# A top-k attention and MLP kernel: output projection as seven half-size products, scores in three PSUM banks, first MLP layer in halves

## The chip, the cores and the metric

The kernel runs on one core of one Trainium2 chip. Its time is the device time of one execution in microseconds, median of several runs; lower is better. The engines are named as the profile names them: PE (matrix products; PEld its weight loads), DVE, ACT, POOL (GpSimd) and SP (which issues the DMAs here). Each works through its own queue in order.

## What is computed

Attention over q, k, v of shape (8, 8, 576, 64), where each query keeps its 32 largest scores, then an MLP of width 2048 over the 4608 x 512 result:

```python
scores = scale * np.matmul(q, k.transpose(0, 1, 3, 2))
kth = np.partition(scores, -top_k, axis=-1)[..., -top_k:-top_k + 1]
scores = np.where(scores >= kth, scores, -1000000000.0)
scores = scores - np.max(scores, axis=-1, keepdims=True)
attn = np.exp(scores)
attn = attn / (np.sum(attn, axis=-1, keepdims=True) + 1e-09)
x = np.matmul(attn, v).transpose(0, 2, 1, 3).reshape(B * S, H * D)
h = x @ w_in
g = h * (1.0 / (1.0 + np.exp(-1.702 * h)))
out = g @ w_out
```

## The kernel before

Work comes in 144 slots, 18 per batch. A slot is 128 queries of two heads at once (`t < NF`, 16 of the 18), or the last 64 queries of four heads (`t == NF`, two of the 18, side by side in a batch; they come first in odd batches and last in even ones). A slot goes through these steps, each a function of the slot's number `n`:

- `scores(n)` (line 221): matmuls of 64 rows of contraction for the two heads in turn, 576 keys each in two parts of 288, into two PSUM tiles `s_ps` of two banks each (the pool has two buffers, four banks). Two ACT copies (line 238) take them to `sc`.
- `topk(n)` (line 240): on the DVE, four rounds of `max` (line 247) and three of `match_replace` (line 250) for each head; 14 instructions.
- `bounds(n)` (line 261): two small POOL instructions that need the end of `topk(n)`.
- `exponentials(n)` (line 269): two Prelu (line 275) and two Exp (line 277) on ACT. `bounds` and `exponentials` together are called `soften`.
- `divide(n)` (line 282): a sum and a reciprocal on the DVE (lines 286, 288), issued after six of the next slot's 14 DVE instructions; then one head is scaled on ACT (line 294) and the other on POOL (line 295).
- `turn_main(n)` and `turn_ends(n)` (lines 318, 322): 8 transposes and 1 transpose on PE (line 306) into banks `tp`, each bank copied to `pt` by ACT (line 316). The pool `ps_t` has two banks for all of `tp` and `o`.
- `values(n)` (line 328): 20 half-width matmuls of attention by v into `o` (line 338; a `t == NF` slot has two `o`), copied by ACT into `xT`. Every fourth slot completes an `xT` of 128 tokens by 512; there are 36 of them.

The MLP of one `xT` is cut in four groups of four 128-wide blocks. `hidden()` (line 372) makes 16 matmuls (line 381) into the bank `ph`; `tanh` (line 393) is an ACT pass over `ph` and a copy of it to `h` (lines 398, 401); `gate` (line 405) makes `gT` from them on POOL (lines 411, 412); `project` (line 419) adds four matmuls of 512 columns (line 429) into the bank `po`, which ACT reads into `ob` after the fourth group (line 434), and SP sends out. Every float32 matmul is two instructions in the profile, a transpose is one.

The order on every engine is the order in which the program is written, under `manual_schedule` (line 640). Slots 0 to 9 run one by one in `slot`, with the weights being loaded and rounded in between; the rest runs in pairs `two_slots(n)` (line 572) for n = 10, 12, ..., 144:

```python
begin(first); soften(n - 1); tanh(aside); find(n); gate(aside)
prepare_some(); middle(n - 2); hidden()
begin(second); soften(n); tanh(aside); gate(aside)
prepare_some(); middle(n - 1); find(n + 1); prepare_some()
# then scores(n + 2), values(n - 2), values(n - 1), scores(n + 3)
prepare_some(); hidden()
```

Here `find` is `topk` with the `divide` of the slot before in it; `middle(m)` is three blocks of a projection, `turn_main(m)`, the fourth block, `turn_ends(m)`; `prepare_some` turns a loaded q or k of two heads (9 transposes for a q and a k, with ACT copies at lines 201 to 208); `begin` issues loads. One group of the first layer and one projection are done per slot; after n = 142 some are left over, which the calls at the end of the program finish.

Of the kernel before, what the change touches and what calls it, by code (L numbers as in the profile page):

```python
# [28 lines left out]
def kernel(  # L29
# [26 lines left out]

    nc = tc.nc
# [16 lines left out]
    FIRST = (TAIL, 0)  # L74
# [5 lines left out]
    SETTLED = 9  # L80
    assert D == 64 and 2 * TAIL == P and C == NP * P and C == PIECE and B % 2 == 0
# [3 lines left out]
    pool = lambda name, bufs, **kw: ctx.enter_context(tc.tile_pool(name=name, bufs=bufs, **kw))  # L85
    raws = pool("raws", 8)
    loads = pool("loads", 2)
# [10 lines left out]
    gtp = pool("gtp", 4)  # L98
    thp = pool("thp", 2)
    osp = pool("osp", 1)  # L100
    ps_s = pool("ps_s", 2, space=PSUM)
# [8 lines left out]


    pieces = [(c, g) for g in range(NG) for c in range(CC)] + [(None, f) for f in range(FC)]
    raw = {}

    def load_piece(n):
        c, g = pieces[n]
        if c is None:
            src = moe_w_out[g * P : (g + 1) * P, :]
        else:
            src = moe_w_in[c * P : (c + 1) * P, g * PIECE : (g + 1) * PIECE]  # L120
        raw[n] = raws.tile([P, 2 * PIECE], U32, name="raw")
        nc.sync.dma_start(raw[n][:], src.bitcast(U32))

    def round_piece(n):
# [9 lines left out]
        dst = wout[:, g, :] if c is None else win[:, c, g * PIECE : (g + 1) * PIECE]  # L134
        words = raw.pop(n)[:].rearrange("p (n w) -> p n w", w=2)
        low, high = words[:, :, 0], words[:, :, 1].bitcast(F32)
# [20 lines left out]

    def stay_warm(count, of=ident[:]):

        none = ps_p.tile([P, C], F32, name="none", tag="po")  # L160
        for i in range(count):
            nc.tensor.matmul(none[:, 0:P], lhsT=of, rhs=of, start=True, stop=True)

    def load(name, b, hp):
        src = q if name == "q" else k
        t = loads.tile([P, NF, 2, D], F32, name=f"{name}_l")
# [3 lines left out]
        if name == "q":  # L170
            loaded["ends", b, hp] = loads.tile([P, 2, D], F32, name="ends")
# [19 lines left out]
    def prepare(name, b, hp):  # L191
        src = loaded.pop((name, b, hp))


        before = 0 if name == "q" else TAIL
        dst = qkt.tile([P, S + before], F32, name=f"{name}_t")
# [4 lines left out]
        nc.scalar.mul(out=dst[:, before : before + FULL], in_=full[:], mul=scale)  # L201
        (qT if name == "q" else kT)[b, hp] = dst
        if name == "k":
# [3 lines left out]
            for to in (0, before + FULL):  # L207
                nc.scalar.copy(out=dst[:, to : to + TAIL], in_=ends[:, TAIL:P])
# [12 lines left out]
    def scores(n):  # L221
        b, t, hps = slots[n]
        ps = [ps_s.tile([P, 2, 512], F32, name="s_ps") for _ in range(2)]
        if t < NF:
            parts = [(i, 0, slice(0, P), slice(t * P, (t + 1) * P)) for i in range(2)]
        else:
            parts = [(i, p, slice(p * TAIL, (p + 1) * TAIL), slice(FULL, S)) for i, p in ((0, 0), (1, 1), (0, 1), (1, 0))]
        for c in range(2):
            for i, p, rows, cols in parts:
                on = slice(i * D, (i + 1) * D)  # L230
                nc.tensor.matmul(  # L231
                    ps[i][rows, c, 0:HALF],
                    lhsT=qT[b, hps[p]][on, cols],
                    rhs=kT[b, hps[p]][on, FIRST[i] + c * HALF : FIRST[i] + (c + 1) * HALF],
                )
        sc = st[n]["sc"] = scp.tile([P, 2, S], F32, name="sc")
        for i in range(2):
            nc.scalar.copy(out=sc[:, i, :].rearrange("p (c k) -> p c k", c=2), in_=ps[i][:, :, 0:HALF])  # L238
# [129 lines left out]
    hidden_at = {"g": 0}  # L368
# [3 lines left out]
    def hidden():  # L372
        if not ready:
            return
        xT, rows = ready[0]
        g = hidden_at["g"]
        ph = ps_h.tile([P, G, P], F32, name="ph")
        for i in range(G):
            f = g * G + i
            for c in range(CC):  # L380
                nc.tensor.matmul(  # L381
                    ph[:, i, :],
# [5 lines left out]
        to_gate.append((ph, g, rows))  # L388
        hidden_at["g"] = (g + 1) % NG
        if g == NG - 1:  # L390
            ready.pop(0)

    def tanh(aside):

        if to_gate:
            ph, g, rows = to_gate.pop()
            th = thp.tile([P, G, P], F32, name="th")
            nc.scalar.activation(th[:], ph[:], AF.Tanh, scale=0.851 / RAISE)  # L398
            if aside:
                h = raws.tile([P, G, P], F32, name="h", tag="raw")  # L400
                nc.scalar.copy(out=h[:], in_=ph[:])
                ph = h
            gated.append((th, ph, g, rows))

    def gate(aside):
        if not gated:
            return
        th, h, g, rows = gated.pop()
        gT = gtp.tile([P, G, P], F32, name="gT")
        if aside:  # L410
            nc.gpsimd.tensor_scalar(th[:], th[:], 1.0, None, op0=ALU.add)  # L411
            nc.gpsimd.tensor_tensor(out=gT[:], in0=th[:], in1=h[:], op=ALU.mult)  # L412
        else:
            nc.vector.scalar_tensor_tensor(
                out=gT[:], in0=th[:], scalar=1.0, in1=h[:], op0=ALU.add, op1=ALU.mult
            )
        to_project.append((gT, g, rows))

    def project(blocks):

        if blocks[0] == 0:
            proj["on"] = to_project.pop(0)
            if proj["on"][1] == 0:
                proj["po"] = ps_p.tile([P, C], F32, name="po")
        gT, g, rows = proj["on"]
        po = proj["po"]
        for i in blocks:
            f = g * G + i
            nc.tensor.matmul(  # L429
                po[:], lhsT=gT[:, i, :], rhs=wout[:, f, :], start=(f == 0), stop=(f == FC - 1)  # L430
# [249 lines left out]
```

## Time and profile before

| | |
|---|---|
| median of 3 runs | 1628.78 us (1628.63 to 1629.83) |
| profiled execution | 1632.4 us |
| its span, first to last instruction | 1630.6 us |
| PE clock granted, mean | 0.987 |
| DMA queues, mean rate | 35 GB/s |
| projection matmuls, L429 | 542.1 us busy, 1152 instructions |
| first-layer matmuls, L381 (`xT`) | 484.6 us busy, 4096 instructions |
| DVE max, L247 (two groups) | 609.9 and 202.2 us busy, 864 and 288 instructions |
| ACT score copies, L238 | 169.9 us busy, 288 instructions |

A busy row counts from an instruction's start to its end, and PE's instructions overlap: L429 has a mean of 594 ns where the next starts after some 430. The time that PE's work takes is therefore read from start to start. In the timeline a row is a start, a length, an engine, a line, an operation, the tiles out and in, the shape, the number of instructions, and the idle time before it with what ended it.

### The profile page before, as it was taken

The page shows a single profiled execution, that of the slowest core. Times are in us where ns is not written, and L with a number is a line of the kernel's source. Part 1 is how long each engine was busy: PE and PEld are TensorE (multiplying, and loading weights), DVE is VectorE, ACT ScalarE, POOL GpSimd, SP SyncE. Part 2 cuts the span into 40 slices and gives each one's busy share as a digit, 9 for nine tenths or more (in the row PEclk, how much of TensorE's full clock was granted, in tenths as well). Part 3 has the DMA queues.
Part 4 walks back from the last instruction along what each step waited for, and adds up shares of the span by engine and source line. Part 5 has one row for each costly group of instructions (what it writes and reads, how often), then busy time and mean ns, then how long its engine had stood idle before and what let it go on. Part 6 is the DMA issues. An engine that isn't in the chain of part 4 may idle for free.

```text
span 1630.6 us, 32137 instructions
## 1 busy us (share of the span) xinstructions
PE 1584.6 (97%) x12025; PEld 1184.1 (73%) x12025; DVE 1479.2 (91%) x3212; ACT 1155.9 (71%) x2449; POOL 754.1 (46%) x782
## 2 busy tenths in 40 slices
PE   7777999999999999999999999999999999999999
PEld 5665677777777777777777777777777777777776
DVE  6998999999999999999999998999999999999960
ACT  5896777777777776677777777777777777777761
POOL 2788344444444444444444444444444444444430
PEclk7898999999999999999999999999999999999999
DMA  7442001110001001110000100111000100000000
GB/s 209 124 137 76 22 22 29 30 43 16 22 15 44 22 23 29 29 37 22 22 15 23 35 17 15 30 30 44 15 22 15 43 22 23 22 8 7 8 8 14
DMA packets 100636, 56.61 MB, mean 35 GB/s; under 512 B 83584, under 2 KB 91776, under 8 KB 100480
## 3 DMA queue, kind: packets, MB, share of 16 engines
q1 hardware_dynamic: 100480, 54.55, 12.1%
q8 instruction: 95, 1.56, 0.4%
q14 instruction: 61, 0.50, 0.1%
HBM read 45.09 MB, written 9.44 MB: 33 GB/s over the span
## 4 chain that ended last, share of the span: by engine, by line
PE 88%; ACT 5%; DVE 4%; POOL 1%; issue 1%; SPq 0%; DMA 0%; POOLq 0%; ACTq 0%
PE ph L381 30%; PE po L429 29%; PE o L338 9%; PE s_ps L231 9%; PE tp L306 8%; DVE top L247 2%; DVE left L250 2%; PE tp L199 1%; ACT sc L238 1%; ACT pr L277 1%; ACT raw L146 1%; PE tp L308 1%; DVE wout L145 0%; ACT sc L275 0%; DMA raw<-in_moe_w_in_dram 0%
## 5 line engine op out<-in xcount | busy, mean ns | idle before, releaser
L247 DVE MAX8 top<-left 128x8 f32<-128x576 f32 x864 | 609.9, 747 | 0.0
L429 PE MATMUL po<-wout,gT 128*128 128x512 f32 x1152 | 542.1, 594 | 0.0
L381 PEld LDWEIGHTS ph<-xT,win 128*128 128x128 f32 x4096 | 467.5, 192 | 41.5 <-issue 40.8
L381 PE MATMUL ph<-xT,win 128*128 128x128 f32 x4096 | 484.6, 277 | 0.0
L250 DVE MATCH_REPLACE8 left<-top,left 128x576 f32<-128x576 f32 x576 | 423.4, 743 | 0.0
L295 POOL TENSOR_SCALAR pr<-pr,rden 128x576 f32<-128x576 f32 x135 | 233.4, 1729 | 356.0 <-ACT th L398 347.9
L411 POOL TENSOR_SCALAR th<-th 128x512 f32<-128x512 f32 x133 | 198.9, 1496 | 224.2 <-ACT th L398 224.2
L429 PEld LDWEIGHTS po<-wout,gT 128*128 128x128 f32 x1152 | 197.8, 191 | 142.3 <-issue 141.8
L275 ACT ACTIVATE sc<-sc,cut 128x576 f32<-128x576 f32 x288 | 208.1, 774 | 130.5 <-POOL cut L266 128.1
L316 ACT COPY pt<-tp 128x512 f32<-128x512 f32 (+1 forms) x432 | 193.2, 481 | 148.1 <-PE tp L306 141.0
L306 PEld LDWEIGHTS tp<-ident,pr 128*128 128x128 f32 x1215 | 145.7, 141 | 113.9 <-issue 65.8
L238 ACT COPY sc<-s_ps 128x576 f32<-128x576 f32 x288 | 169.9, 644 | 75.8 <-PE s_ps L231 75.4
L277 ACT ACTIVATE pr<-sc,low 128x576 f32<-128x576 f32 x288 | 219.2, 764 | 0.0
L247 DVE MAX8 top<-sc 128x8 f32<-128x576 f32 x288 | 202.2, 744 | 11.3 <-ACT sc L238 11.3
L250 DVE MATCH_REPLACE8 left<-top,sc 128x576 f32<-128x576 f32 x288 | 211.7, 743 | 0.0
L306 PE MATMUL tp<-ident,pr 128*128 128x128 f32 x1215 | 177.7, 273 | 9.0 <-ACT q_t L201 7.7
L231 PE MATMUL s_ps<-k_t,q_t 64*128 64x288 f32 (+1 forms) x1280 | 183.3, 433 | 0.9 <-ACT k_t L201 0.9
L412 POOL TENSOR_TENSOR gT<-th,h 128x512 f32<-128x512 f32 x133 | 169.8, 1277 | 11.1
L338 PE MATMUL o<-pt,v_l 128*64 128x128 f32 (+1 forms) x2560 | 158.9, 267 | 1.2 <-ACT pt L316 0.3
L338 PEld LDWEIGHTS o<-pt,v_l 128*64 128x64 f32 x2560 | 131.6, 138 | 31.3 <-ACT pt L316 15.8
L231 PEld LDWEIGHTS s_ps<-k_t,q_t 64*128 64x128 f32 (+1 forms) x1280 | 100.0, 178 | 59.6 <-issue 40.5
L266 POOL TENSOR_SCALAR cut<-top 128x2 f32<-128x2 f32 x144 | 38.2, 265 | 208.5 <-DVE top L247 206.8
(55 smaller groups left out, 1175.3 us busy)
## 6 DMA issues: line engine op xcount, KB each, us to landing
q_l<-in_q_dram SPq DMA_DIRECT2D x64, 128.0 KB, 2.9
k_l<-in_k_dram SPq DMA_DIRECT2D x64, 128.0 KB, 2.9
raw<-in_moe_w_in_dram SPq DMA_DIRECT2D x16, 512.0 KB, 5.1
v_l<-in_v_dram SPq DMA_DIRECT2D x32, 256.0 KB, 3.0
raw<-in_moe_w_out_dram SPq DMA_DIRECT2D x16, 512.0 KB, 3.3
out_dram<-ob SPq DMA_DIRECT2D x32, 256.0 KB, 2.3
ends<-in_q_dram SPq DMA_DIRECT2D x32, 32.0 KB, 2.4
ends<-in_k_dram SPq DMA_DIRECT2D x32, 32.0 KB, 2.6
```

Source lines behind the costliest of these rows:

```text
L231: nc.tensor.matmul(ps[i][rows, c, 0:HALF], lhsT=qT[b, hps[p]][on, cols], rhs=kT[b, hps[p]][on, FIRST[i] + c * HALF : FIRST[i] + (c + 1) * ...
L247: nc.vector.max(top[:, i, 8 * r : 8 * r + 8], (left if r else sc)[:, i, :])
L250: nc.vector.match_replace(left[:, i, :], top[:, i, 8 * r : 8 * r + 8], (left if r else sc)[:, i, :], LOWEST)
L275: nc.scalar.activation(sc[:, i, :], sc[:, i, :], AF.Prelu, bias=cut[:, i : i + 1], alpha=HUGE)
L277: nc.scalar.activation(pr[:, i * S : (i + 1) * S], sc[:, i, :], AF.Exp, bias=low[:, i : i + 1], accum_out=den[:, i : i + 1],)
L295: nc.gpsimd.tensor_scalar(pr[:, S : 2 * S], pr[:, S : 2 * S], rden[:, 1:2], None, op0=ALU.mult)
L306: nc.tensor.transpose(tp[:, c * P : (c + 1) * P], pr[:, at], ident[:])
L316: nc.scalar.copy(out=to, in_=tp[:, 0 : blocks * P])
L338: nc.tensor.matmul(o[j * D : (j + 1) * D, 0 : cols.stop - cols.start], lhsT=main[:, j, c, :] if c < NF else tail[:, j, :], rhs=pt[:, j * N ...
L381: nc.tensor.matmul(ph[:, i, :], lhsT=win[:, c, f * P : (f + 1) * P], rhs=xT[:, c, :], start=(c == 0), stop=(c == CC - 1),)
L411: nc.gpsimd.tensor_scalar(th[:], th[:], 1.0, None, op0=ALU.add)
L429: nc.tensor.matmul(po[:], lhsT=gT[:, i, :], rhs=wout[:, f, :], start=(f == 0), stop=(f == FC - 1))
```

## The change

**Projection.** The 128 tokens, the 512 output columns and the 2048 wide contraction are each cut in halves, and the product is made from seven products of halves, by Strassen's scheme. A group now holds blocks 2g, 2g+1 of the first half of the contraction and the same of the second (`blocks_of`), and the weights are loaded in that order. Sums and differences of the left side go into `th`, those of the weights (`tees`) are made once. `po` takes four strips of 256 columns, two banks. Products that are 64 tokens wide stand two by two in the lower and upper half of the partitions. `gather` reads all to SBUF, with the halves swapped where needed, and `combine` adds them up.

```diff
+    def differences(gT, th, on):
+        s = th[:].rearrange("p s (j t) -> p s j t", j=2)
+        part = lambda row, col: gT[:, 2 * col : 2 * col + 2, row * TAIL : (row + 1) * TAIL]
+        for to, x, y, op in (
+            (s[:, 0], part(1, 0), part(1, 1), ALU.add),
+            (s[:, 1], s[:, 0], part(0, 0), ALU.subtract),
+            (s[:, 2], part(0, 0), part(1, 0), ALU.subtract),
+            (s[:, 3], part(0, 1), s[:, 1], ALU.subtract),
+        ):
+            on.tensor_tensor(out=to, in0=x, in1=y, op=op)
...
+    def t_one(to):
+        half = C // 2
+        for f in range(0, FC // 2, 2):
+            on = wout[:, f : f + 2, half:]
+            to.tensor_tensor(out=on, in0=on, in1=wout[:, f : f + 2, 0:half], op=ALU.subtract)
+    def project_seven():
...
+        for j in range(2):
+            f = 2 * g + j
...
+            runs += [
+                (0, 0, gT[:, j, 0:TAIL], near[:, 0:half], j),
+                (0, 1, s[:, 1, j, :], tee[0], j),
+                (1, 0, s[:, 0, j, :], near[:, half:], j),
+                (1, 1, s[:, 2, j, :], tee[1], j),
+                (2, 0, gT[:, 2 + j, 0:TAIL], far[:, 0:half], j),
+                (2, 1, gT[:, 2 + j, TAIL:P], tee[2], j),
+            ]
+        runs += [(3, j, s[:, 3, j, :], wout[:, FC // 2 + 2 * g + j, half:], None) for j in range(2)]
+        for k, side, left, right, j in runs:
+            nc.tensor.matmul(
+                po[side * TAIL : (side + 1) * TAIL, k, :],
...
+    def gather(po):
+        e = place["products"]
+        x = osp.tile([P, 2, C // 2], F32, name="x", tag="ob")
+        nc.scalar.mul(out=e, in_=po[:], mul=mul)
+        for to, at, src, k in ((low, 0, high, 0), (high, 0, low, 0), (low, 1, high, 3), (high, 1, low, 1)):
+            nc.scalar.mul(out=x[to, at, :], in_=po[src, k, :], mul=mul)
+        return e, x
+    def combine(e, x, rows, to):
+        for out_, a, b_ in (
+            (x[:, 0, :], x[:, 0, :], e[:, 0, :]),
+            (e[:, 1, :], e[:, 1, :], x[:, 0, :]),
+            (e[low, 2, :], e[low, 2, :], e[low, 0, :]),
+            (e[high, 2, :], e[high, 2, :], e[high, 1, :]),
+            (x[:, 1, :], x[:, 1, :], e[:, 1, :]),
+            (x[low, 1, :], x[low, 1, :], e[low, 3, :]),
+        ):
+            to.tensor_tensor(out=out_, in0=a, in1=b_, op=ALU.add)
+        for on, where in rows:
+            nc.sync.dma_start(where[:, 0 : C // 2], e[on, 2, :])
+            nc.sync.dma_start(where[:, C // 2 : C], x[on, 1, :])
```

It is switched on (`mode["seven"]`) in the pair n = 20, where the oldest waiting group is the first of a block; the old four-block product does the groups before.

**Scores.** `s_ps` becomes one tile of three banks, with one buffer. The first 512 keys of each head are two matmuls of 128 and 384 columns; the last 64 keys of both heads are one matmul of 128 columns over all 128 rows, against a block-diagonal tile `k_e` (six of them, set to zero at the start). One ACT copy of 1152 elements takes both heads, in place of two of 576.

```diff
-    ps_s = pool("ps_s", 2, space=PSUM)
+    ps_s = pool("ps_s", 1, space=PSUM)
...
+        def main():
+            for start, stop in ((0, P), (P, FULL)):
...
+        def ends():
+            for p, rows, cols in blocks:
                 nc.tensor.matmul(
+                    ps[rows, FULL : S + TAIL], lhsT=qT[b, hps[p]][:, cols], rhs=kends[b, hps[p]][:],
                 )
+        for do in (ends, main) if ends_first else (main, ends):
+            do()
...
+        for i in (slice(0, 2),) if n else (slice(0, 1), slice(1, 2)):
+            nc.scalar.copy(
+                out=sc[:, i, :].rearrange("p i k -> p (i k)"), in_=ps[:, i.start * S : i.stop * S]
+            )
```

**First layer and the order of a pair.** `hidden_half(i)` makes two of the four blocks of a group, `tanh` and the copy to `h` follow for that half, and the transposes of a slot stand between the halves. The loads of q and k share three buffers instead of two each. The pair is written anew:

```diff
+        def layer(m, at):
+            where = at if aside else None
+            for i in range(2):
+                hidden_half(i)
+                if aside:
+                    tanh(at, i)
+                if turning(m):
+                    (turn_ends if i else turn_main)(m)
...
+        soften(n - 1)
+        if n > SETTLED + 1 and tees_left:
+            for _ in range(4):
+                tees_left.pop(0)()
+        while extras:
+            extras.pop(0)()
+        layer(n - 2, 0)
+        prepare_some()
+        find(n)
+        gate()
+        layer(n - 1, 1)
         prepare_some()
+        begin(second_todo)
+        if not mode["seven"] and n >= SEVEN and not tees_left and to_project and to_project[0][2] == 0:
+            mode["seven"] = True
+            t_one(nc.gpsimd)
+            for gT, th, g, rows in to_project:
+                differences(gT, th, nc.gpsimd)
...
+        if not mode["seven"]:
+            for _ in range(take):
+                project(range(G))
+        scores(n + 2, slots[n + 2][1] < NF)
         soften(n)
+        for m in (n - 2, n - 1):
+                values(m)
+        if fresh:
+            differ()
+        find(n + 1)
+        if mode["seven"]:
+            done = [project_seven() for _ in range(take)]
+        gate()
...
+                e, x = gather(po)
+                if aside:
+                    extras.append(lambda: combine(e, x, rows, nc.gpsimd))
...
+        if live(n + 3):
+            scores(n + 3, slots[n + 3][1] == NF)
         prepare_some()
```

`take` is 2 in a full pair, so a pair projects the two groups whose first layer ran in the pair before it. `extras` holds the differences of the second group and, every other pair, `combine`; both are run on POOL at the start of the next pair, after `bounds(n - 1)`. After the last slot the DVE does this work.

## Prediction

> **What bounds the kernel now.** I read the page's busy shares, then its slices, then one pair of slots in the timeline, engine by engine. A "pair" is one pass of `two_slots`; the 67 that begin with n = 10, 12 ... 142 are most of the run.
>
> ```profile
> span 1630.6 us, 32137 instructions
> PE 1584.6 (97%) x12025; PEld 1184.1 (73%) x12025; DVE 1479.2 (91%) x3212; ACT 1155.9 (71%) x2449; POOL 754.1 (46%) x782
> PE   7777999999999999999999999999999999999999
> DVE  6998999999999999999999998999999999999960
> 300.00:1500.00 1200.00, 1199.50 (x9210) 895.60 (x9209) 1135.94 (x2477) 867.98 (x1851) 547.51 (x562) 1.00 0.09 24
> L412 POOL TENSOR_TENSOR gT<-th,h 128x512 f32<-128x512 f32 x133 | 169.8, 1277 | 11.1
> ```
>
> The window row (PE, PEld, DVE, ACT, POOL) shows PE busy for 1199.5 of 1200 us, DVE for 1135.9. Busy PE rows can hide gaps, so I took the starts in one pair that prepares no q or k:
>
> ```profile
> 673.08 2.74 PE L429 MATMUL po<-wout,gT 128*128 128x512 f32 x6
> 675.65 1.04 PE L306 MATMUL tp<-ident,pr 128*128 128x128 f32 x8
> 676.53 1.02 PE L429 MATMUL po<-wout,gT 128*128 128x512 f32 x2
> 677.39 0.27 PE L306 MATMUL tp<-ident,pr 128*128 128x128 f32 x1
> 677.59 1.24 PE L231 MATMUL s_ps<-k_t,q_t 64*128 64x288 f32 x8
> 678.76 1.09 PE L338 MATMUL o<-pt,v_l 128*64 128x128 f32 x16
> ...
> 681.10 1.24 PE L231 MATMUL s_ps<-k_t,q_t 64*128 64x288 f32 x8
> 682.27 3.84 PE L381 MATMUL ph<-xT_t,win 128*128 128x128 f32 x32
> 685.94 2.74 PE L429 MATMUL po<-wout,gT 128*128 128x512 f32 x6
> ...
> 690.36 3.74 PE L381 MATMUL ph<-xT_t,win 128*128 128x128 f32 x32
> 693.93 0.59 PE L429 MATMUL po<-wout,gT 128*128 128x512 f32 x1
> ```
>
> From start to start: projection 2 x (2.57 + 0.86) = 6.87, transposes 2 x (0.88 + 0.11, with 0.1 at a change of shape) about 2.0, scores 2 x 1.17, values 2.34, first layer 3.67 + 3.57 = 7.24. The sum is 20.8; the pair took 20.85. There is no wait in it: PE's own work is the bound. Over the run a pair takes 21.32 us (the DVE's first pass of n = 12 starts at 168.56, of n = 142 at 1554.33; 65 pairs), the rest being prepares, some 0.45 of PE.
>
> The DVE has little room: one half of a pair without a wait is 10.25 us (671.45 to 681.70), the other about 9.9, so some 20.15 per pair. What ACT does at a pair's start matters below:
>
> ```profile
> 682.42 1.18 ACT L238 COPY sc<-s_ps 128x576 f32<-128x576 f32 x2 [0.94 <-PE s_ps L231]
> 683.49 1.45 ACT L275 ACTIVATE sc<-sc,cut 128x576 f32<-128x576 f32 x2
> 684.83 0.77 ACT L277 ACTIVATE pr<-sc,low 128x576 f32<-128x576 f32 x1
> ...
> 686.35 0.58 ACT L398 ACTIVATE th<-ph 128x512 f32<-128x512 f32 x1
> 689.15 1.07 ACT L316 COPY pt<-tp 128x512 f32<-128x512 f32 x2 [1.07 <-PE tp L306]
> ```
>
> Softening (L275, L277) holds ACT for 2.86 us, 683.49 to 686.35. Before the change PE passes a whole first-layer call and three projection blocks between the score matmuls and the first transpose; the `pt` copy waits for PE.
>
> **What the Trainium skill says.** "TensorEngine Tiling (Array Packing)", Key Properties: tiles of the array can load and multiply in parallel, and a change of tiling mode drains it. The trace agrees: 20 half-width matmuls of 128 columns pass in 1.17 us (59 ns each), 8 full-width transposes in 0.88 (110 each). "TensorE: Matmul & The Clock Gate", Step-by-step: matmuls stay in program order and only weight loads are pulled ahead; so a waiting transpose holds all behind it (the trace has one of 7.73 us at 162.56). "SBUF — State Buffer", Who interferes with whom: a DVE instruction with one SBUF input does not contend with GpSimd. L247 stays between 734 and 760 ns all run, so I charge POOL's new work nothing on the DVE's searches. "GPSIMD Engine Reference", 3.1, calls two-input arithmetic on GpSimd about twice as slow as on the DVE; the rows here give 1277 ns (L412) against 685 (L414), and I price from them.
>
> **PE work, part by part.** Projection: 7 products, each over two 128-row blocks per group, give 14 matmuls of 256 columns, two side by side: 7 x 256 = 1792 columns for 4 x 512 = 2048. So 3.44 becomes 3.01 a group; a pair's two cost 6.05 with one change of shape, -0.82. If the halves did not overlap it would be 12. Scores: 128 + 384 columns and a 128-column last part are 640 for 576, so 1.17 + 0.11 = 1.28 twice, +0.22. Halves of the first layer, values and transposes keep their columns. Net -0.60 (bounds -0.4 to -0.75): 20.25 for this pair, close to the DVE's 20.15. Without a new wait, that is all the gain there can be.
>
> **What the new order makes PE wait for.** Call p the time when PE finishes `scores(n+3)`. PE then does half a layer 1.8, eight transposes 0.87, half a layer 1.8, and stands at p+4.5 before `turn_ends`, which needs a third `tp` bank of two. That bank comes free by the first `pt` copy. ACT's queue up to there: the score copy from p+0.2 (1152 elements at the slope of 512 to 576, 1.0), softening 2.86, half a tanh and half an h copy (256 elements, about 0.27 each), the `pt` copy 0.59: p+5.2, and PE goes on at p+5.3. That is **+0.8 in every pair** (0.5 to 1.0), and a later or earlier start of the pair doesn't shorten it, as the chain starts from PE's own last score matmul. It alone eats the gain.
>
> Every second pair ends an output block. `gather` stands on ACT ahead of the copy of `scores(n+3)`: 1024 elements 0.9 and four of 256 about 1.05. It starts when the products end, p-1.1, so the score copy starts at p+0.85 rather than p+0.2: +0.65. In the pair after it POOL has the differences (4 x 0.47, from 202 ns at 2 elements and 1277 at 512) and `combine` (6 x 0.74) ahead of the divide that the second head's transposes need: POOL is free some 7.1 after the DVE's start, divides until 8.85, and PE is there at 8.2; prepares cover part. I take +0.5 (0 to 1.2). The same POOL queue then brings `bounds(n)` about 1 late; that shows on the DVE, which has slack as long as PE is behind.
>
> Slots of sequence ends (one pair per batch, 6 of them in this stage) have four `o` tiles on the two `tp` banks. The third needs the first copied; that copy now stands behind `soften(n)` on ACT. After the score matmuls: copy 1.2, softening 2.86, copy 0.25 is 4.35, where PE needs it at 1.2: **+3.1 each**, 0.30 a pair. Before the change the same wait was 0.20 us (PEld L338 on ACT xT_t at 658.92).
>
> A steady pair: -0.60 + 0.80 + (0.65 + 0.50)/2 + 0.30 = +1.08; 61 pairs (n = 22 to 142): **+66**.
>
> **Start.** Before `mode["seven"]` (n = 10, 12, 16, 18) two or more old projections, 3.44 each, stand on PE ahead of `scores(n+2)`, and `soften(n)` now stands behind that copy on ACT. In n = 16: layers and turns to p+10, projections to 16.9, scores 18.2, copy 19.4, softened at 22.3; the DVE wants it at 14.3 after its start. With DVE and PE in their worst places that is 6 each for 16 and 18, 7 for 10, 2 for 12. At n = 20 POOL has `t_one` (4 x 1.3) and three sets of differences (3 x 1.9) ahead of `bounds`: 8. Sum 29; some of it replaces the 4.30 and 1.65 us waits of the DVE around 160 now. I take **+25** (8 to 35). The six zero tiles on POOL (0.2 each), the third buffer for q and k loads instead of four, and weight pieces in two runs lie beside the opening's DMA waits: 0, up to 3.
>
> **End.** 6 first-layer calls and 8 projections remain after n = 142, against 5 and 9; the last block adds gather, combine on the DVE and a second DMA, and one product waits for a gather: **+6** (0 to 12). In between SP issues twice the output DMAs; it is mostly idle, 0. ACT gets 22 us less by one score copy per slot (0.15 each), and halves of tanh add that back; only its order counts.
>
> Sum: 1630.6 + 66 + 25 + 6 = 1727.6 of span. The profiled execution took 1632.4, 1.8 over its span, and the median of the runs, 1628.78, is 3.6 below that: **1726**.
>
> **Rivals.** (a) The likeliest, as above, with the bounds of its terms 1685 to 1765: chance 0.44. (b) The waits are half as long (turn_ends 0.4, no POOL lateness, start 12, end 3): 61 x (-0.60 + 0.40 + 0.33 + 0.30) + 15 = +41, about 1669; chance 0.21. For it: durations at ACT are pipelined, a prepare at the pair's end gives ACT time. (c) The other side: the first `pt` copy is done before PE needs the third bank. It decides from a chain of 4.5 us instead of 5.3. Then PE's work sets the pace until the DVE does: 61 x -0.60 = -37, start +4: 1595; chance 0.26. For it: ACT is busy 71% and has time on average; against it: it is a queue in order, and softening is in front. (d) POOL (13.6 to 18 us a pair, from 10) becomes the pace where strided or half-partition operands cost more than 2.1 ns per element: another 1 per pair, 1790; 0.07. (e) The 64-wide products do not overlap: +6 a pair, about 2080; 0.02, the values rows speak against it.
>
> No change to within 0.2% (3 us, about what a measurement of this kernel can tell) lies between (b) and (c), 0.03. Faster 0.25, slower 0.72. The range reaches from (c) into (d): 1593 to 1765.
>
> **What would show it.** Right: PE no longer full; transposes of `turn_ends` waiting for ACT's `pt` copy some 0.8 us in each pair; weight loads of `o` waiting about 3 us for ACT once in nine pairs; pairs of 21.5 and 22.7 by turns; PE's product rows at 3.0 us a group. Wrong: PE still gapless with pairs near 20.7, or a `pt` copy that waits for PE; then (c). A product group of more than 3.2 us would break the gain's size, `bounds` late on POOL in all pairs would mean (d).

## The result: 1979 us, and the profile after

The changed kernel takes 1979.35 us (median of four runs, 1972.27 to 1981.23) against 1629.3 us for the kernel before in the same runs (1628.63 to 1630.31): 1.214 times as long, 95% interval 1.211 to 1.217. The forecast had the sign, but 1726 us and a range to 1765 us. The profiled execution of the changed kernel spans 1970.5 us.

The first lines of its page, and two groups of its table (busy time and mean ns of one; idle time just before, and what ended it):

```profile
span 1970.5 us, 39302 instructions
PE 1665.5 (85%) x14985; PEld 1335.3 (68%) x14985; DVE 1476.9 (75%) x3249; ACT 1222.9 (62%) x2701; POOL 1116.9 (57%) x1492
PEclk7997888999999999999999999989999999999999
L422 PE MATMUL ph<-xT,win 128*128 128x128 f32 x4096 | 550.8, 291 | 181.3 <-ACT raw L451 175.6
L551 PE MATMUL po<-wout,gT 128*64 128x256 f32 x1056 | 298.5, 385 | 2.8 <-ACT x L568 2.8
```

PE was full before and is now 85% busy, and the clock row is not all nines in the middle of the run. The idle time stands before the first layer (L422), and what ends it is L451, ACT's copy of a finished half of that layer. The seven products (L551) hardly wait. Over the middle stretch of the next table PE stands idle for 199.4 us, 175.0 of them before L422 until L451.

Where the 339.9 us of span come from, by the DVE's first pass of slots 22 and 142:

| stretch | before | after | more | forecast |
|---|---|---|---|---|
| start, to slot 22 | 276.5 | 341.0 | 64.5 | 25 |
| 60 pairs, 22 to 142 | 1277.8 | 1538.7 | 261.0 | 65 |
| from slot 142 to the end | 76.3 | 90.7 | 14.4 | 6 |

The middle stretch, first before and then after, as window rows (length, busy us of PE, PEld, DVE, ACT and POOL, then the granted clock):

```profile
276.54:1554.33 1277.79, 1277.29 (x9798) 953.62 (x9796) 1211.55 (x2641) 922.57 (x1962) 583.50 (x600) 1.00 0.09 24
```

```profile
340.99:1879.74 1538.75, 1339.34 (x12507) 1086.72 (x12504) 1196.74 (x2642) 983.86 (x2202) 916.35 (x1261) 0.96 0.08 20
```

PE idles 199 us of the stretch, where it idled half a microsecond. Its busy time is 62 us longer. These two numbers are the 261 us. Nearly all of the 62 is the clock: the trace has 119 us at half the clock here, and PE was busy for 112 of them; if work takes twice as long at half the clock (an estimate), that is 56 us.

A plain pair of the changed kernel, without preparation and without a gather, on PE's timeline (start, length; in brackets the wait before and what ended it):

```profile
1008.89 1.95 PE L422 MATMUL ph<-xT,win 128*128 128x128 f32 x16
1010.68 1.04 PE L346 MATMUL tp<-ident,pr 128*128 128x128 f32 x8
1013.70 2.05 PE L422 MATMUL ph<-xT,win 128*128 128x128 f32 x16 [1.99 <-ACT raw L451]
1015.59 0.27 PE L346 MATMUL tp<-ident,pr 128*128 128x128 f32 x1
1016.49 2.05 PE L422 MATMUL ph<-xT,win 128*128 128x128 f32 x16 [0.63 <-ACT raw L451]
```

and ACT over the same time:

```profile
1009.15 1.12 ACT L276 COPY sc<-s_ps 128x1152 f32<-128x1152 f32 x1 [4.61 <-PE s_ps L268]
1010.16 1.45 ACT L315 ACTIVATE sc<-sc,cut 128x576 f32<-128x576 f32 x2
...
1013.02 0.36 ACT L449 ACTIVATE th<-ph 128x256 f32<-128x256 f32 x1
1013.29 0.36 ACT L451 COPY raw<-ph 128x256 f32<-128x256 f32 x1
1013.54 1.08 ACT L356 COPY pt<-tp 128x512 f32<-128x512 f32 x2
```

The second half of the layer is not ready to go at 1011.55, when the transposes end: it starts at 1013.70, when ACT has copied the first half out. That copy stands where the forecast put it, behind the copy of the scores and the softening. What the forecast did not see is that PE waits for it at all. Once it has waited, the transposes of the ends (1015.59) find their bank free, and the 0.8 us forecast for them doesn't occur. The first half of the next layer (1016.49) then waits another 0.63 us in the same way.

PE's time in this pair, from start to start by line, sums to 23.54 us against 20.86 before: transposes with the waits behind them 4.93 for 2.06, products 6.14 for 6.87, scores 2.78 for 2.34, first layer 7.45 for 7.25, values 2.23 for 2.33. Without the two waits (2.61) that is 20.93: PE's own work is no less than before.

The next pair follows a gather and takes 27.37 us. Its PE rows and two windows in it:

```profile
1034.22 1.04 PE L346 MATMUL tp<-ident,pr 128*128 128x128 f32 x8
1038.35 2.53 PE L422 MATMUL ph<-xT,win 128*128 128x128 f32 x16 [3.09 <-ACT raw L451]
...
1041.61 3.79 PE L422 MATMUL ph<-xT,win 128*128 128x128 f32 x16 [0.52 <-ACT raw L451]
```

```profile
1038.30:1041.60 3.30, 2.75 (x17) 2.34 (x17) 3.30 (x7) 1.65 (x5) 3.13 (x4) 0.72 0.26 87
1041.60:1046.70 5.10, 5.09 (x24) 5.09 (x25) 5.10 (x12) 1.86 (x5) 4.61 (x8) 0.51 0.49 111
```

The gather lengthens the wait from 1.99 to 3.09 us, and after it the granted clock is at half: half a layer takes 3.58 us to the next start instead of 1.8. Other gather pairs have the longer wait but keep their clock; they take 24.65 us. So a gather costs 1.1 us, and the fall of the clock 2.7 us where it comes.

### The profile page after: what moved, and what is told of

Its sections match the earlier page's. It is cut to its first block, busy times and chain, and to the rows that moved or that the text cites. A ratio compares the mean times of both kernels' runs of the same rounds, so it can differ in the third digit from the quotient of the medians.

```text
span 1970.5 us, 39302 instructions
## 1 busy us (share of the span) xinstructions
PE 1665.5 (85%) x14985; PEld 1335.3 (68%) x14985; DVE 1476.9 (75%) x3249; ACT 1222.9 (62%) x2701; POOL 1116.9 (57%) x1492
## 4 chain that ended last, share of the span: by engine, by line
PE 53%; ACT 25%; DVE 12%; issue 5%; POOL 4%; DMA 1%; SPq 0%; ACTq 0%; POOLq 0%; DVEq 0%
PE ph L422 22%; PE po L551 13%; ACT pr L317 9%; DVE left L290 6%; DVE top L287 5%; PE o L378 5%; ACT sc L276 4%; PE s_ps L260 4%; PE tp L346 4%; ACT sc L315 3%; POOL th L480 2%; ACT x L568 2%; ACT raw L451 2%; ACT th L449 2%; PE po L491 2%
## 5 line engine op out<-in xcount | busy, mean ns | idle before, releaser
L422 PE MATMUL ph<-xT,win 128*128 128x128 f32 x4096 | 550.8, 291 | 181.3 <-ACT raw L451 175.6
L422 PEld LDWEIGHTS ph<-xT,win 128*128 128x128 f32 x4096 | 511.3, 203 | 219.3 <-ACT raw L451 200.1
L326 DVE TENSOR_SCALAR some<-den 128x2 f32<-128x2 f32 x144 | 26.7, 186 | 424.9 <-ACT pr L317 424.9
L551 PE MATMUL po<-wout,gT 128*64 128x256 f32 x1056 | 298.5, 385 | 2.8 <-ACT x L568 2.8
L276 ACT COPY sc<-s_ps 128x1152 f32<-128x1152 f32 (+1 forms) x145 | 161.1, 1112 | 222.4 <-PE s_ps L268 154.9
L449 ACT ACTIVATE th<-ph 128x256 f32<-128x256 f32 (+1 forms) x276 | 107.4, 389 | 297.6 <-PE ph L422 297.6
L551 PE MATMUL po<-raw,th 128*64 128x256 f32 x1056 | 276.8, 385 | 0.0
L551 PE MATMUL po<-wout,th 128*64 128x256 f32 x1056 | 239.1, 382 | 0.0
L551 PEld LDWEIGHTS po<-wout,gT 128*64 128x64 f32 x1056 | 144.6, 139 | 72.6 <-issue 3.6
L463 POOL TENSOR_TENSOR gT<-th,raw 128x512 f32<-128x512 f32 x132 | 168.6, 1278 | 24.1 <-PE po L551 12.9
```

Source lines behind the costliest of these rows:

```text
L276: nc.scalar.copy(out=sc[:, i, :].rearrange("p i k -> p (i k)"), in_=ps[:, i.start * S : i.stop * S])
L422: nc.tensor.matmul(ph_all[:, j, :], lhsT=win[:, c, f * P : (f + 1) * P], rhs=xT[:, c, :], start=(c == 0), stop=(c == CC - 1),)
L551: nc.tensor.matmul(po[side * TAIL : (side + 1) * TAIL, k, :], lhsT=left, rhs=right, start=(g == 0 and j == 0 and k in (0, 2)), stop=(g == ...
```

## The experiments

All times are medians; ratios are to the kernel before, run on the same chip, with 95% intervals.

**Are the seven products the cost? (e1)** The four old blocks in their place; no differences, gather or combination, and no sums of the weights made beforehand.

```diff
-        if mode["seven"]:
-            done = [project_seven() for _ in range(take)]
+        if n >= SEVEN + 2:
+            for _ in range(take):
+                project(range(G))
```

> The change without its seven products: the old four-block product stands where the seven products stand, with no differences, gather or combine; all else as changed. Theory G (the halves of the first layer wait for ACT's reads of the other half, about 3.0 us a pair, and longer waits behind gather drop PE's clock): every pair without a prepare takes about 24.4 us (23.54 + 0.82), none 27, the clock stays at 1.0; near 1925 us. Theory S (the seven products themselves are what costs): pairs return to about 21.5 and the time to under 1700 us.

2059.81 us, 1.263 (1.260 to 1.267): 80 us slower without the seven products. A plain pair grows from 23.54 to 24.57, as the products (6.14 us) give way to blocks of about 7.06. The half clock, which the first theory did not expect, comes more often: most plain pairs take 27.27, and the clock of the middle stretch is 0.92. The start is unchanged (slot 22 at 341.6), so GpSimd's preparation of the weights costs nothing there that shows. The products are a gain in this order of work, but a small one: with their gather every second pair takes 24.65, so at the full clock two pairs average 24.1 against 24.57. Most of the 80 us is the clock: over the middle stretch what it loses is at most 135 us here (a clock of 0.917 over 1628.2 us) and at most 60 in the changed kernel (0.961 over 1538.7).

**What is the wait for: the bank, the tile, or ACT? (e2, e5)** With one bank of `po` free again, e2 puts the halves of the first layer of e1 into two banks of one tile, and e5 into two tiles of one bank each. Between these two the matmuls, the copies and the number of banks are the same.

```diff
-    ph_all = ps_h.tile([P, G, P], F32, name="ph")
+    ph_two = ps_h.tile([P, 2, 512], F32, name="ph")
+    ph_half = [ph_two[:, i, 0 : 2 * P].rearrange("p (j t) -> p j t", j=2) for i in range(2)]
...
```

and from e2 to e5:

```diff
-    ph_two = ps_h.tile([P, 2, 512], F32, name="ph")
-    ph_half = [ph_two[:, i, 0 : 2 * P].rearrange("p (j t) -> p j t", j=2) for i in range(2)]
+    ph_two = [ps_h.tile([P, 512], F32, name=f"ph{i}") for i in range(2)]
+    ph_half = [ph_two[i][:, 0 : 2 * P].rearrange("p (j t) -> p j t", j=2) for i in range(2)]
```

> As the run with four blocks, and the two halves of the first layer stand in two PSUM banks (the bank that the old product leaves free), in one tile. Theory G by bank: the second half no longer waits for ACT, what is left is the wait before turn_ends (0.8 us); a pair without a prepare is near 22.3 us, the time near 1800 us. If the wait goes by the tile, or is ACT being late whatever PE does, nothing changes: 24.4 us and 1925 us.

> The four-block projection of e1 with the halves of the first MLP layer in two tiles of their own, one PSUM bank each (e2 had two banks in one tile and left the waits of 1.99 and 0.63 us as they were). If the wait goes by the tile, the second half no longer waits for ScalarE's copy of the first: about 2.4 us less in a pair, which leaves the wait of some 0.8 us ahead of the transposes of the ends: pairs of 22.2 us, and with the granted clock back near 0.97 a time of about 1880 us. If ScalarE is only late, the second half starts at once and the transposes of the ends, which wait for a copy that stands behind tanh and copy of both halves, take the wait over: pairs stay near 24.5 us and the time near 2050 us.

e2: 2053.26 us, 1.259 (1.256 to 1.263), within 0.4% of e1. e5: 1816.12 us, 1.114 (1.112 to 1.116), 237 us less than e2. PE in e2:

```profile
1155.71 1.04 PE L347 MATMUL tp<-ident,pr 128*128 128x128 f32 x8
1158.73 2.81 PE L423 MATMUL ph<-xT,win 128*128 128x128 f32 x16 [1.99 <-ACT raw L454]
```

and in e5:

```profile
1007.70 1.04 PE L347 MATMUL tp<-ident,pr 128*128 128x128 f32 x8
1008.57 1.95 PE L423 MATMUL ph<-xT,win 128*128 128x128 f32 x16
1011.21 0.33 PE L347 MATMUL tp<-ident,pr 128*128 128x128 f32 x1 [0.69 <-ACT pt L357]
```

The wait follows the tile: two banks of one tile keep it at 1.99 us, two tiles end it. Freed of it, PE waits 0.69 us ahead of the transposes of the ends: the very wait that the forecast had reckoned as 0.8. Plain pairs take 22.19 us, as the expectation had it, and the time is lower than its 1880 us; the clock stays at 0.99 over the middle stretch (0.92 in e2). Of the 237 us, 214 lie in the middle stretch, 15 before slot 22 and 9 after slot 142.

In the changed kernel itself the halves share a tile and a bank. e2 and e5 show that a shared tile is enough for the wait; what a shared bank would do alone is not shown. Scores hold three banks there, transposes two, the seven products two and the first layer one; a second bank for it would be a ninth, and no kernel here has more than eight. Two tiles in that one bank were not tried: the Trainium skill, "PSUM — Partial Sum Buffer", section "PSUM bank collisions raise a hardware error", says that PE writing and ACT reading one bank in the same partitions at once is an error. No run here shows it.

**The layer whole (e3)**

```diff
-            for i in range(2):
-                hidden_half(i)
-                if aside:
-                    tanh(at, i)
-                if turning(m):
-                    (turn_ends if i else turn_main)(m)
+            hidden()
+            if aside:
+                tanh(at)
+            if turning(m):
+                turn_main(m)
+                turn_ends(m)
```

> The change with the first layer whole again: 32 matmuls in a row, then tanh and the copy over the whole bank, then the transposes; seven products kept. Theory G: one wait in place of two in each layer, at turn_ends (1.4 and 0.9 us a pair): pairs of 22.9 and about 24 us instead of 23.5 and 27.4, clock near 0.98, some 1850 us. Theory S: no change beyond 1%, about 1970 us.

1929.04 us, 1.183 (1.180 to 1.187): 50 us better, but not the 1850 expected. The wait for the first half is gone, and another has come in its place, ahead of the transposes of the ends: 1.11 and 0.78 us in a plain pair, which takes 22.60, and 2.22 and 0.78 in one after a gather, which takes 23.7 or, with the clock down, 25.3. In one after a gather:

```profile
1016.50 1.04 PE L346 MATMUL tp<-ident,pr 128*128 128x128 f32 x8
1019.75 0.33 PE L346 MATMUL tp<-ident,pr 128*128 128x128 f32 x1 [2.22 <-ACT pt L356]
```

The copies of the transposes now stand behind tanh and copy of the whole layer. Neither way of cutting the layer hides ACT's queue in this order of the pair.

**How much is the clock? (e4)** Ten matmuls that compute nothing, before the second half in the pairs after a gather.

```diff
+                if i and fill:
+                    stay_warm(fill)
                 hidden_half(i)
```

> The change with ten idle matmuls put in front of the second half in each pair that follows a gather (useless work, 2.2 us, in the place where PE stands idle for 3.1 us). If the clock's fall after that idle time costs what I think (2.5 to 2.9 us in every second pair), such pairs go from 27.4 to about 24.7 us, the clock to 0.98 and the time to about 1895 us. If the clock does not matter, the time stays at 1975 us or rises by up to 10.

1957.65 us, 1.201 (1.196 to 1.206): useless work makes it about 20 us faster, not 80. Those pairs fall from 27.37 to 24.67 mostly, as expected, but the clock then falls in some others that kept it; over the middle stretch it is 0.98 instead of 0.96. So the clock is a cost of its own, and the smaller one: the waits that let it fall remain.

**The start (e6, e12)** In pair 10 of the changed kernel, the DVE and PE:

```profile
185.99 0.17 DVE L326 TENSOR_SCALAR some<-den 128x2 f32<-128x2 f32 x1 [22.98 <-ACT pr L317]
```

```profile
157.93 1.12 PE L491 MATMUL po<-wout,gT 128*128 128x512 f32 x2 [4.04 <-POOL wout L163]
160.54 2.07 PE L491 MATMUL po<-wout,gT 128*128 128x512 f32 x2 [1.48 <-POOL wout L163]
```

e6 softens slot n ahead of the scores of slot n + 2. e12 is e6 with the last pieces of the weights put earlier on GpSimd.

```diff
+        soften(n)
         if live(n + 2):
             scores(n + 2, slots[n + 2][1] < NF)
-        soften(n)
...
-                if i > 5 and unfinished:
+                if i > 1 and unfinished:
```

> The changed kernel with the softening of slot n put ahead of the scores of slot n + 2, so that ScalarE's softening doesn't stand behind the copy of these scores. Theory of the start: the 22.98 us that VectorE waits in pair 10, and part of those of pairs 12 to 20, come from this order; the start loses 15 to 35 us and the steady pairs, whose length TensorE's waits set, stay at 25.6 us: about 1950 us. Rival: the start is late because the projection waits for GpSimd's last pieces of the weights, and the order costs nothing: 1975 to 1985 us. A second rival: the copy of the scores comes 2.9 us later and the next scores wait for their one buffer: over 2000 us.

> e6 with the last pieces of the output weights put on GpSimd after the third of VectorE's passes, as in the kernel before, and not after the seventh. In the changed kernel the projection of pair 10 waits 4.04, 1.48, 0.53 and 0.52 us for these pieces. If they are what is left of the late start, pair 10 loses some 5 to 7 us and the steady part nothing: about 1948 us. Rival: GpSimd's two passes of 2.65 us for each piece set the pace wherever they stand, and the division of slot 9 comes behind them: no change from e6's 1955 us, or some us more.

e6: 1954.9 us, 1.199 (1.196 to 1.202); slot 22 comes at 320.9 instead of 341.0. e12: 1942.62 us, 1.192 (1.185 to 1.198); slot 22 at 313.9, pair 10 in 24.8 us instead of e6's 34.8. The intervals of the two ratios overlap, so it is the traces, one of each, that tell e12 from e6. By them both causes are real. Of the 64.5 us of a late start, the order accounts for 20 and the pieces for 7. Some 15 belong to the halves in one tile (slot 22 at 325.8 in e5, 340.4 in e2). What is left is gone in e8 below.

**The scores alone (e7)** The kernel before with the three-bank scores and nothing else of the change.

```diff
-    ps_s = pool("ps_s", 2, space=PSUM)
+    ps_s = pool("ps_s", 1, space=PSUM)
...
-        ps = [ps_s.tile([P, 2, 512], F32, name="s_ps") for _ in range(2)]
+        ps = ps_s.tile([P, 3 * 512], F32, name="s_ps")
```

> The kernel before with nothing of the change but the scores in three banks with the block-diagonal last part (its own projection, whole first layer, order of the pair). The sum of the prediction: 0.22 us a pair on TensorE, 14 us over 66 pairs, and the one buffer hidden by the products of the values: about 1643 us. Rival: the one copy of 1.11 us in the place of two of 0.64 lets the softening begin later or earlier, and VectorE's wait of 1.58 us for the exponentials moves with it: 1625 to 1660 us. Rival for the study: if the one buffer of scores is itself what costs, over 1700 us.

1649.04 us, 1.012 (1.010 to 1.013), 18.8 us more; plain pairs 21.10 for 20.86. The net is as forecast (0.24 for 0.22), but two errors meet in it: the scores themselves take 2.78 us a pair for 2.34, which is 0.44 more, and the first layer and the transposes beside them 0.10 less each. The one buffer brings no wait of note: PE is idle for 0.1 us of the middle stretch.

**The sevens in the old order (e8, e9, e11, e10)** e8 keeps all the arithmetic of the change but goes back to the whole layer and to the old order of the pair, with the softening first on ACT:

```diff
+            if live(m) and "pr" in st[m]:
+                turn_main(m)
+            if go and seven:
+                got = project_seven()
+            if between:
+                between()
+            if live(m) and "pr" in st[m]:
+                turn_ends(m)
```

> All three parts of the change but with the first layer whole and in the order of the kernel before: transposes, seven products of one group, transposes of the ends, whole layer; the softening first on ScalarE; the copy of the scores of slot n + 3 put off until the next pair's projection; the differences and the combination in GpSimd's gaps. If the seven products are sound and the order of the changed kernel is what costs, TensorE's 20.86 us of a pair become 20.86 - 0.86 + 0.22 = 20.2, VectorE's two searches of 10.08 set the pair at 20.2 to 20.6 us, and the time is 1600 to 1615 us, faster than before. If the gather, the differences and the combination cost by themselves, pairs with a gather come out at 22 us or more and the time is over 1640 us.

1777.81 us, 1.091 (1.089 to 1.093): 200 us less than the changed kernel, and slot 22 at 279.4, within 3 us of the kernel before. e8 changes the order, the layer and the place of the weight pieces together, so it does not tell which of them held what was left of the late start. Plain pairs reach 20.27 us by the DVE's marks, as expected, but each is followed by one with a gather of 21.92: 21.1 on average, where the kernel before takes 20.86. Pairs with a preparation take 23.4 to 29.1, and PE shows why, here in one with a gather too:

```profile
1013.80 1.14 PE L260 MATMUL s_ps<-k_t,q_t 64*128 64x128 f32 x8 [1.65 <-ACT sc L278]
1014.87 0.68 PE L268 MATMUL s_ps<-k_e,q_t 128*128 128x128 f32 x2
1015.35 5.21 PE L426 MATMUL ph<-xT,win 128*128 128x128 f32 x32
```

A wait of 1.65 us, and a whole layer takes 5.21 us instead of 3.7, at half the clock from 1015.03 on. On ACT the gather before it had waited for the send of the row before (`[1.17 <-DMA out_dram<-raw]`). e9 moves three things to take such waits away:

```diff
             if live(m) and "pr" in st[m]:
                 turn_main(m)
+            while left_over:
+                left_over.pop(0)()
...
-        on_the_side(2)
+        on_the_side(3)
...
-        prepare_some()
-        middle(n - 2)
+        middle(n - 2, prepare_some)
```

> e8 with three moves: the combination's six additions and its sends within one pair of the gather (e8's gather waited 1.17 us for the send of the row before); the preparation of q and k behind the seven products, so that its copies don't stand ahead of those of the transposes; the put-off copy of the scores behind the copies of the first transposes. In e8 a pair with neither a gather nor a preparation took 20.27 us, one with a gather alone 21.92 and those with both 24 to 29 us, with the clock at half after waits of 1.65 and 2.80 us. If these waits are the whole of it, pairs become 20.3 to 21.3 us and the time 1600 to 1625 us. Rival: the gather's 2.6 us of ScalarE and the preparation can't be had in one pair, whatever the order: the pairs with both stay over 24 us and the time over 1700 us.

1681.91 us, 1.031 (1.029 to 1.033). The clock holds 1.00 in the middle stretch and the long pairs shrink to 21 to 24 us, between the two theories. In a pair with a gather the DVE still waited:

```profile
1315.72 1.56 ACT L572 ACTIVATE x<-po 64x256 f32<-64x256 f32 x4
1317.31 1.12 ACT L278 COPY sc<-s_ps 128x1152 f32<-128x1152 f32 x1
```

```profile
1318.53 1.42 DVE L291 MAX8 top<-sc 128x8 f32<-128x576 f32 x2 [1.90 <-POOL th L484]
```

The row names GpSimd, but the search reads `sc`, whose copy behind the gather ends at the same instant. e11 puts these scores ahead of the seven products, so that their copy goes first:

```diff
             while left_over:
                 left_over.pop(0)()
+            if ahead:
+                ahead()
...
+            lambda: live(n + 2) and scores(n + 2, slots[n + 2][1] < NF),
```

> e9 with the scores of slot n + 2 ahead of the second seven products of the pair, so that their copy stands ahead of the gather on ScalarE. In e9 VectorE waits 1.9 us for that copy in a pair with a gather, and 1.65 to 3.84 us in pairs with preparations. If these waits set the length of those pairs, a pair with a gather falls from 21.8 to 20.9 us, which is TensorE's own work, and one with preparations to 22 to 23 us: 1640 to 1660 us. Rival: TensorE is as late in those pairs as VectorE, and VectorE's wait only shows it: the time stays at 1675 to 1690 us. In both cases not faster than before, since TensorE's pair is 20.87 us in e9 and 20.86 before.

1680.2 us, 1.031 (1.029 to 1.033), no different from e9: the rival was right. The wait for `sc` is gone, and one for the exponentials has taken its place; in the lists of waits (total, times, longest), e9 and then e11:

```profile
DVE some L330 <- ACT pr L321: 33.1, 26, 8.3
```

```profile
DVE some L330 <- ACT pr L321: 131.2, 70, 8.3
```

PE has no gap from 1294 to 1344 us of e11, which hold no preparation; there the DVE only waits for a busy PE. e10 puts both groups of a pair in one place:

```diff
+            done = [project_seven()] if take else []
+            if turning(n - 2):
+                turn_ends(n - 2)
...
+            if take:
+                done.append(project_seven())
```

> e9 with both seven-product groups of a pair in one place, parted only by the transposes of the ends, and the scores of slot n + 2 and their copy ahead of the products of the values. In e9 the sevens take 6.34 us a pair beside 6.88 for the four blocks and the scores 0.24 more, so TensorE's pair is 20.87 us there, no less than in the kernel before; a pair with a gather was 21.8 because the copy of the scores stood behind the gather's 2.6 us on ScalarE and VectorE waited 1.9 us for it. If the sevens gain when they stand together and the copy comes in time, pairs take 20.3 to 20.6 us, 0.4 more with a preparation, and the time is 1605 to 1635 us, no slower than before. Rival: what the seven products save on TensorE is used up by scores, transposes and gather in any order: pairs stay at 21 us or more with those of a gather longer, and the time is 1650 to 1690 us.

e10 leaves out one thing: the differences of every second group are formed only after its products have been made. The instructions and their sizes are the same, and only its time is used. 1691.81 us, 1.038 (1.036 to 1.040): the rival again. PE is without a gap in a plain pair, which still takes 21.4 us from start to start; the transposes, set between the products of the values, take 2.54 for 2.06 and the values 2.49 for 2.33.

No version with the seven products beat the kernel before. In e9 and e11 they take 6.34 us a pair, their two groups in two places, against 6.87 for the blocks. That 0.53 is used up on PE itself: scores 2.78 for 2.34, transposes, between other shapes, 2.26 for 2.06, first layer 7.15 for 7.25. A pair of e11 without preparation comes to 20.87 us on PE, and one of the kernel before to 20.86. So on PE alone the three parts together save nothing, even where nothing waits. The 34 us by which e11's middle stretch is longer than before (1311.9 for 1277.8) lie elsewhere: PE is busy for 7.6 us more and idle for 26.5 more, mostly in 36 waits of 0.58 us for ACT's copies of a prepared q or k. No run takes these away.

## Why the prediction was right in its sign and wrong in its size

**The step that failed** is in "What the new order makes PE wait for": "PE then does half a layer 1.8, eight transposes 0.87, half a layer 1.8, and stands at p+4.5 before `turn_ends`". The second half does not start until ACT has read the first, because both are one tile, `ph_all`. In place of the 0.8 us stands a wait of 1.99 us, and 0.63 at the next layer. e5 against e2, with the old blocks, shows that this is the cause, and its price there: 237 us with the clock it drags down. The forecast's own chain on ACT was right, and in e5, where the halves are apart, its 0.8 shows as 0.69. It reckoned when the copy would be done and asked only the third bank of the transposes who waits for it; it should have asked every buffer that ACT reads in that stretch.

**PE's own work** was the second term to fail, and it lies outside its stated bounds: forecast -0.60 (-0.4 to -0.75), measured +0.07 (20.93 for 20.86). The products are near it, -0.73 for -0.82. The scores are +0.44 for +0.22, in every kernel that has them: 1.39 us a slot where the forecast has 1.28, and what is missing is about the 0.1 us that it charges elsewhere for a change of shape. First layer and transposes, taken as unchanged, are +0.20 and +0.25, which comes with the waits: in e5, where the halves don't wait, they are +0.06 and -0.04. The values are -0.10.

**The clock** was in none of the terms. The gap of each pair was priced at its own length. By the estimate above the clock adds 56 us, 0.9 a pair.

**The sum of a steady pair**, forecast +1.08, measured +4.35: PE's own work +0.07 for -0.60; the waits 2.6 at the halves for 0.80 at the ends; the gather's +0.65 was 1.1, and the +0.50 for a late GpSimd doesn't show, since a gather pair with its clock is just 1.1 longer. Together they were forecast 0.58 a pair and are 0.55, by luck, as one error cancels the other. The waits of slots at sequence ends, forecast 3.1 each, are 2.90, six times in this stretch: 0.29 a pair for 0.30. With the clock's 0.9 that is 4.4; the pairs with preparations wait a little less.

**Start**, +25 forecast, 64.5 measured: the mechanism named, `soften(n)` behind the copy of later scores, is right and gives 20 (e6). Not seen was that the projection, moved to the head of the pair, runs into weight pieces still on GpSimd, moved to later passes (7 us, e12), nor that the halves wait here too (15 us, e5 against e2). The 8 us for `t_one` at slot 20 don't show (e1). **End**, +6 forecast, 14.4 measured; no run took it apart, but in e9's order it is 79.7 against 76.3.

**The rivals**: (c), faster at 1595, had for it that ACT has time on average; the first wait of every pair decides against it. (d), GpSimd as the pace, is not seen: no wait of PE in the middle stretch ends at GpSimd, and the DVE is busy no longer (1196.7 us for 1211.6) although GpSimd is (916 for 584). (e), products that don't overlap, is out: two groups pass in 6.14 us. That its 2080 us lies nearer to the measured time than the forecast does is chance.

## What to carry to other kernels

Cutting a step in halves let the other engine begin earlier here only when the halves were tiles of their own (e5); count the PSUM banks for that before counting the gain. Price a new order by asking, for each buffer an in-order engine has yet to read, who is about to write it. A saving of some 3% on the bound engine is small beside one wait of 2 us a pair, and smaller still if the wait brings the clock down. Charge a change of shape wherever one is added: here such small terms used up the whole saving on PE.

## What the runs showed of the hardware that was not expected

The granted clock falls after short waits. The Trainium skill, "TensorE: Matmul & The Clock Gate", Part 1, describes a free-running window of about 3.4 us, and its section "Why this matters for your kernels" warns of gaps of more than about 3 us. The traces agree on the window: in the middle stretches the clock is at half for 3.41 us or a multiple of it, and all these stretches of a run begin on one grid of 3.41 us. They do not agree on the gap: a wait of 1.99 us (e2) and, once, of 1.65 us (e8) was followed by the half clock.

Laid on that grid, the traces show what counts: PE's idle time within one window. The middle stretches (slots 22 to 142) of all fourteen traces have 5562 windows at the full clock. Each of the 223 with more than 1.95 us of idle PE was followed by the half clock, and of those with less than 1.90 us only three were, the one of e8 among them. This is why the same wait brings the fall in one pair and not in the next. The changed kernel has 27 waits of 3.09 us in its middle stretch. In 14 of them one window holds 1.96 us of the wait or more, and the clock fell; in the other 13 the grid cuts the wait into parts of at most 1.92 us, and it did not. The half clock goes on where PE then waits for 0.52 us or more of the next window (92 windows) and ends where it waits 0.44 us or less (235); three windows at 0.52 ended it too. PE's ends are modelled in the profile, so the edges are as rough as that. So a kernel near them has pairs of two lengths, 24.65 and 27.37 us here.
